# Windowed attention in a fused attention, MoE and FFT-FFN kernel: from two heads a product to rows of 128 queries of one head

## Chip, cores and metric

The kernel runs on one core of one Trainium2 chip. The metric is the device time of one execution in microseconds (us), the median of three runs.

## The reference

Three stages follow one another on inputs of 2 batches, 8 heads, 768 positions and head size 64. The change lies in the first:

```python
scores_l = scale * q @ k.T              # scale = 1/8; kept where |i-j| < 16, else -1e9
k_sum = k.reshape(B,H,24,32,D).max(3)   # one key for each block of 32
v_sum = v.reshape(B,H,24,32,D).mean(3)
scores_s = scale * (q . k_sum) + log(32)
a = softmax(concat([scores_l, scores_s], -1))   # sum + 1e-9 below the line
out = a @ concat([v, v_sum])
```

The second stage is a mixture of 8 experts (each token one expert, chosen by its logits or taken over from the token before it), the third a two-dimensional Fourier transform with a layer norm and a feed-forward network.

## The kernel before

**Attention** (`attention`, from L49). A unit u is a batch and four of its heads (hg); there are four units. A unit is cut into six steps c, a step into two blocks j of 64 queries, so that there are 24 steps t = 6u+c, each with 128 queries of four heads. A block of 64 queries needs 96 keys of its window and the 24 block keys, 120 in all. The loop at L208 runs over t and takes the phases of five steps at once, so that all engines have work:

- S1 (L123, TensorE) forms the scores of step t. Two heads share a product: their queries lie on the partitions 0 to 63 and 64 to 127 of a tile Q that is zero elsewhere, so one product has 128 rows of the contraction and 128 output rows (64 queries of the first head, 64 of the second) by 120 columns. There are four products a step; each shows as two weight loads and two matmuls in the trace.
- D1 (L130, VectorE) adds the mask and takes the negative maximum, four times a step on 128x120 (a custom instruction and one that reads its accumulator).
- A1 (L138, ScalarE) takes the exponential, four times.
- S3 (L144) transposes (four times), A3 (L149) copies the result to `att`.
- S4 (L151) multiplies by the values: four products of 128 columns of `att` by 130 columns (two heads, each with 64 values and a 1 that gives the sum). Only the half of each result that belongs to its own head is used.
- D4 (L159, VectorE) takes the reciprocals of the sums and scales: four reciprocals on 64x2 and four multiplications on 64x128.
- S5, A5, S6 (L178 to L190) transpose the finished rows and multiply them by the router's weights into the PSUM tile `big`.

At step t the TensorE does S1(t), S6(t-5), S3(t-2), S4(t-3) and S5(t-4), in this order; the VectorE does D1(t), then D4(t-3); the ScalarE A3(t-2), A5(t-4), A1(t). The queues run in program order. S1 has two PSUM buffers (`psc`), S4 three (`ppo`).

Around them lies the preparation of the next unit, set out by step in the tables PREP and LOADS (L203 to L205): `prep_q` copies the queries into Q (ScalarE, GpSimd), `prep_k` takes the block maxima (L98) and copies them behind each window (L99), both on the VectorE, `prep_v` adds up the values of a block (L109, GpSimd), and `prep_v2`, `prep_v3` bring them to their rows behind the values (L120). SyncE issues the loads of a unit one to five steps ahead. All of it needs the data of unit u+1 from DMA.

From step 13 on, pieces of the router's work (the generator `early`) are put between the VectorE's instructions by `ex.d()` and on the TensorE by `ex.p()`, up to eight and one a step. After step 28 the router's second part follows, in which the VectorE and TensorE answer each other, then the experts.

Of the kernel before, what the change touches and what calls it, by code (L numbers as in the profile page):

```python
# [15 lines left out]
def keep_warm(nc,I,ps,n):  # L16
    """matrix products without a use, that keep the tensor engine's clock up while it waits"""
    for _ in range(n): nc.tensor.matmul(ps,lhsT=I['busy'][:,0:128],rhs=I['busy'],start=True,stop=True)

def lay_attn(q,k,v,wg,wl):  # L20
    c=np.ascontiguousarray
    # b hg h2 d pair j q'
# [11 lines left out]
    band=(np.abs(qq+16-r)<16)  # L34
    m=np.full((3,128,120),np.log(32.0)*8,np.float32)
    for vi in range(3):
        bb=band.copy()
        if vi==1: bb&=(r>=16)
        if vi==2: bb&=(r<80)
        w=np.where(bb,0.0,-8e9)  # L40
        m[vi,:64,:96]=w; m[vi,64:,:96]=w
    mask=c(m.transpose(1,0,2))
# [6 lines left out]
def attention(tc,ctx,cp,I,ident,x_dram,plg,late,hook,ex):  # L49
    """plg psum [128,2hg,12,10]"""  # L50
    nc=tc.nc
    with tc.tile_pool(name="at2",bufs=2) as p2, tc.tile_pool(name="at1",bufs=1) as p1, \
         tc.tile_pool(name="at3",bufs=3) as p3, ExitStack() as pctx, \
         tc.tile_pool(name="pat",bufs=1,space=PSUM) as pat_, \
         tc.tile_pool(name="ppo",bufs=3,space=PSUM) as ppo_, tc.tile_pool(name="pxt",bufs=1,space=PSUM) as pxt_:
        px_=pctx.enter_context(tc.tile_pool(name="atx",bufs=1)); sctx=ExitStack(); psc_=sctx.enter_context(tc.tile_pool(name="psc",bufs=2,space=PSUM,side="right"))
        mask=p1.tile([128,3,120],F32,name="mask"); 
        wgl=p1.tile([128,4,10],F32,name="wgl"); 
        Q=[p1.tile([128,2,12,2,64],F32,name=f"Q{i}") for i in range(2)]
        nc.vector.memset(Q[0][0:64,:,:,1,:],0.0); nc.vector.memset(Q[0][64:128,:,:,0,:],0.0)  # L60
# [4 lines left out]
        kw={};vw={};vT={};qt={};KS={}  # L65
        kw[0]=p2.tile([128,2,12,120],F32,name="kw0",tag="kw",bufs=3)
        k0=p2.tile([128,2,12,120],F32,name="k0",tag="kw",bufs=3).rearrange("p a b c -> p (a b c)")[:,0:1664].rearrange("p (a b) -> p a b",a=2)
        def load(u,what):
# [18 lines left out]
        def prep_q(u,pr,h2,eng):  # L87
            s=slice(64*h2,64*h2+64); eng(Q[u%2][s,pr,:,h2,:],qt[u][s,pr])
        def prep_q0(js,k=0):
            for j in js:  # L90
                for h2 in range(2):
                    s=slice(64*h2,64*h2+64)
                    (nc.scalar.copy if (h2+k)%2==0 else nc.vector.tensor_copy)(Q[0][s,:,j,h2,:],qt[0][s,:,j])
        def prep_k(u,pr,half=None):
            o=slice(0,12) if half is None else slice(6*half,6*half+6)
            if half in (None,0): KS[u,pr]=p3.tile([128,24],F32,name=f"ks{u}_{pr}",tag="ks")
            ks=KS[u,pr]
            nc.vector.tensor_reduce(ks.rearrange("p (j t) -> p j t",j=12)[:,o],kw[u][:,pr,o,16:80].rearrange("p j (t r) -> p j t r",t=2),axis=AX.X,op=ALU.max)  # L98
# [12 lines left out]
        def prep_v2(u):
            pv=pxt_.tile([120,2,128],F32,name=f"pv{u}",tag="xt")
            for pr in range(2): nc.tensor.transpose(pv[:,pr,:],vs[u%3][:,pr,:],ident)
            vv=vss[u%2][96:120].rearrange("p (c e) -> p c e",e=65)[:,:,0:64]
            nc.scalar.mul(vv,pv[96:120].rearrange("p a (h d) -> p (a h) d",h=2),1.0/32)
            src=vss[u%2][96:121].unsqueeze(1)
            row=lambda j,k: vw[u][96:121,j:k].rearrange("p j c e -> p j (c e)")
            prep_v3(u,nc.scalar.copy,0,2)
        def prep_v3(u,eng,j,k):
            eng(vw[u][96:121,j:k].rearrange("p j c e -> p j (c e)"),vss[u%2][96:121].unsqueeze(1).to_broadcast([25,k-j,260]))  # L120
        xt={}; st={}
        NT=24
        def S1(t):  # L123
            u,c=divmod(t,6)
            sc=psc_.tile([128,512],F32,name=f"sc{t}",tag="sc")[:,0:480].rearrange('p (g k) -> p g k',g=4)
            for g in range(4):
                jj,pr=divmod(g,2); j=2*c+jj
                nc.tensor.matmul(sc[:,g,:],lhsT=Q[u%2][:,pr,j].rearrange('p a b -> p (a b)'),rhs=kw[u][:,pr,j,:],start=True,stop=True)
            st['s',t]=sc
        def D1(t):  # L130
            u,c=divmod(t,6); sc=st.pop(('s',t))
            e=p2.tile([128,4,120],F32,name=f"e{t}",tag="e"); nm=p3.tile([128,4],F32,name=f"nm{t}",tag="nm")
            for g in range(4):
                j=2*c+g//2; vi=1 if j==0 else 2 if j==11 else 0
                nc.vector.tensor_tensor_reduce(out=e[:,g,:],in0=sc[:,g,:],in1=mask[:,vi,:],scale=-0.125,scalar=1e30,op0=ALU.add,op1=ALU.min,accum_out=nm[:,g:g+1])
                if t>16: ex.d()
            st['e',t]=(e,nm)
        def A1(t):  # L138
            e,nm=st.pop(('e',t))
            a=p3.tile([128,4,120],F32,name=f"a{t}",tag="a")  # L140
            for g in range(4):
                nc.scalar.activation(a[:,g,:],e[:,g,:],AF.Exp,bias=nm[:,g:g+1],scale=-1.0)
            st['a',t]=a
        def S3(t):  # L144
            a=st.pop(('a',t))
            pa=pat_.tile([120,4,128],F32,name=f"pa{t}",tag="pa")
            for g in range(4): nc.tensor.transpose(pa[:,g,:],a[:,g,:],ident)
            st['pa',t]=pa
        def A3(t):  # L149
            nc.scalar.copy(att[t%2][0:120],st.pop(('pa',t)))  # L150
        def S4(t):  # L151
            u,c=divmod(t,6); b,hg=U[u]
            for jj in range(2):
                po=ppo_.tile([128,2,130],F32,name=f"po{t}_{jj}",tag="po")
                for pr in range(2):
                    j=2*c+jj
                    nc.tensor.matmul(po[:,pr,:],lhsT=att[t%2][0:121,2*jj+pr,:],rhs=vw[u][:,j,2*pr:2*pr+2,:].rearrange("p a b -> p (a b)"),start=True,stop=True)
                st['po',t,jj]=po
        def D4(t):  # L159
            u,c=divmod(t,6); b,hg=U[u]  # L160
            if hg==0: xt[(b,c)]=px_.tile([128,512],F32,name=f"xt{b}_{c}",tag=f"xt{c}")
            x=xt[(b,c)]
            xv=x.rearrange("p (g a h d) -> p g a h d",g=2,a=2,h=2)
            rs=p3.tile([128,2,2],F32,name=f"rs{t}",tag="rs")
            pos=[st.pop(('po',t,jj)) for jj in range(2)]
            for jj in range(2):
                for h2 in range(2):
                    s=slice(64*h2,64*h2+64)
                    nc.vector.reciprocal(rs[s,jj],pos[jj][s,:,65*h2+64])
            for jj in range(2):  # L170
                for h2 in range(2):
                    s=slice(64*h2,64*h2+64)
                    nc.vector.tensor_tensor(out=xv[64*jj:64*jj+64,hg,:,h2,:],in0=pos[jj][s,:,65*h2:65*h2+64],
                        in1=rs[s,jj].unsqueeze(2).to_broadcast([64,2,64]),op=ALU.mult)
                    if t>12: ex.d()
            if hg==1:
                nc.sync.dma_start(x_dram[b*896+c*128:b*896+c*128+128],x)
        def S5(t):  # L178
            u,c=divmod(t,6); b,hg=U[u]
            px=pxt_.tile([128,2,128],F32,name=f"px{t}",tag="xt")  # L180
            for i in range(2): nc.tensor.transpose(px[:,i,:],xt[(b,c)][:,hg*256+i*128:hg*256+i*128+128],ident)
            st['px',t]=px
        def A5(t):
            xT=p2.tile([128,2,128],F32,name=f"xT{t}",tag="xT")
            nc.scalar.copy(xT,st.pop(('px',t)))
            st['x',t]=xT
        def S6(t):
# [826 lines left out]
```

## Time and profile before

| | us |
|---|---|
| median of three runs | 624.75 |
| lowest, highest | 623.68, 631.16 |
| span of the profiled execution | 627.5 |

The profiled execution has no time of its own in the list; of the three runs only the one of 631.16 is as long as its span. The span runs from the first to the last instruction. The stages on it: attention up to 115 us, the router's second part to 148, experts to 283, transform to 346, feed-forward to the end. A duration in the trace is that of one instruction from its start to its end; matmuls overlap, so what one costs in a row is read from the distance of the starts.

### The profile page before, as it was taken

To read this page: it belongs to the slowest core of one execution; us is meant where nothing else is said; L and a number is where in the kernel's file an instruction comes from. 1 tells how busy PE (TensorE), PEld (TensorE's weight loads), DVE (VectorE), ACT (ScalarE), POOL (GpSimd) and SP (SyncE) were. 2 spreads that over 40 slices of the span, in tenths; PEclk is the share of its full clock that TensorE was granted. 3 is DMA by queue.
4 is the path that set the end of the run, shared out by engine and by line. 5 is a ranking of instruction groups with operands and counts; after the bars stand their busy time and mean duration, and the time that the engine had idled before them with its cause. 6 is when DMAs were issued, how large, how long until landed. Compare 5 with 4: busy or idle time off the path is not lost.

```text
span 627.5 us, 8719 instructions
## 1 busy us (share of the span) xinstructions
PE 574.5 (92%) x3154; PEld 487.1 (78%) x3154; DVE 388.8 (62%) x944; ACT 252.3 (40%) x472; POOL 159.1 (25%) x166
## 2 busy tenths in 40 slices
PE   7788788669999999996989999879999999999997
PEld 4688778658998899995858787657888888888885
DVE  5898988784989898882686999992311111311012
ACT  4675746424566767662425434444112111111000
POOL 5631225454044344331265323430000000000000
PEclk8897989889999999997978999998999999999999
DMA  8994305407898899923301434420100000100001
GB/s 253 335 324 168 111 6 217 184 21 281 304 341 271 332 361 309 311 110 103 135 0 33 153 117 134 145 91 1 67 1 1 0 2 0 68 0 1 0 1 67
DMA packets 21933, 84.05 MB, mean 134 GB/s; under 512 B 2782, under 2 KB 3294, under 8 KB 18304
## 3 DMA queue, kind: packets, MB, share of 16 engines
q1 hardware_dynamic: 18432, 72.62, 33.3%
q0 software_dynamic: 3456, 10.85, 4.9%
q8 instruction: 26, 0.43, 0.3%
q14 instruction: 19, 0.16, 0.1%
HBM read 73.23 MB, written 10.22 MB: 133 GB/s over the span
## 4 chain that ended last, share of the span: by engine, by line
PE 37%; DVE 15%; issue 1%; ACT 1%; SPq 0%; DMA 0%; DVEq 0%
PE fpy L923 16%; PE fph L912 15%; DVE ft L683 3%; DVE ft L684 2%; DVE ft L682 2%; PE s1q L800 1%; DVE fhl L915 1%; DVE st L727 1%; DVE ft L681 1%; PE lpt L756 1%; PE py L553 1%; PE ph L539 1%; PE s L800 1%; DVE cl L778 1%; PE pp L800 0%
## 5 line engine op out<-in xcount | busy, mean ns | idle before, releaser
L915 DVE SCALAR_TENSOR_TENSOR fhl<-fph,fhh 128x512 fp32r<-128x512 f32 x48 | 33.1, 689 | 143.7 <-ACT fhh L914 143.7
L914 ACT ACTIVATE fhh<-fph 128x512 fp32r<-128x512 f32 x48 | 28.6, 596 | 156.4 <-PE fph L912 156.4
L539 PE MATMUL ph<-xx,wh 128*128 128x256 f32 x448 | 84.4, 290 | 6.1 <-DMA dwr<-x_dram 6.1
L923 PE MATMUL fpy<-fwh,fhl 128*128 128x512 f32 x192 | 76.3, 397 | 6.2 <-DVE fhl L915 6.2
L539 PEld LDWEIGHTS ph<-xx,wh 128*128 128x128 f32 x448 | 72.3, 196 | 8.2 <-issue 6.5
L912 PE MATMUL fph<-unh,fwh 128*128 128x512 f32 x192 | 76.1, 396 | 0.0
L923 PE MATMUL fpy<-fwh,fhh 128*128 128x512 f32 x192 | 76.0, 396 | 0.0
L923 PE MATMUL fpy<-fwl,fhh 128*128 128x512 f32 x192 | 75.6, 394 | 0.0
L912 PE MATMUL fph<-unh,fwl 128*128 128x512 f32 x192 | 75.5, 393 | 0.0
L912 PE MATMUL fph<-unl,fwh 128*128 128x512 f32 x192 | 75.5, 393 | 0.0
L539 PE MATMUL ph<-xx,wl 128*128 128x256 f32 x224 | 64.5, 288 | 0.8 <-DVE wl L530 0.8
L530 DVE TENSOR_TENSOR wl<-wr,wh 128x1024 fp32r<-128x1024 f32 x47 | 55.4, 1220 | 12.5 <-ACT wh L529 12.5
L529 ACT CAST wh<-wr 128x1024 fp32r<-128x1024 f32 (+1 forms) x58 | 56.2, 1018 | 15.9 <-PE py L553 13.5
L689 POOL TENSOR_TENSOR fwl<-ft,fwh 128x512 fp32r<-128x512 f32 x32 | 43.2, 1351 | 75.1 <-ACT fwh L688 75.0
L923 PEld LDWEIGHTS fpy<-fwh,fhl 128*128 128x128 f32 x192 | 36.3, 189 | 16.6 <-DVE fhl L915 8.8
L553 PE MATMUL py<-wh,hl 128*128 128x512 f32 x112 | 44.6, 398 | 4.8 <-DVE hl L544 4.8
L539 PEld LDWEIGHTS ph<-xx,wl 128*128 128x128 f32 x224 | 44.3, 198 | 1.2 <-DVE wl L530 1.2
L553 PE MATMUL py<-wh,hh 128*128 128x512 f32 x112 | 45.2, 404 | 0.0
L553 PE MATMUL py<-wl,hh 128*128 128x512 f32 x112 | 44.2, 394 | 0.0
L923 PEld LDWEIGHTS fpy<-fwl,fhh 128*128 128x128 f32 x192 | 36.5, 190 | 8.1
L912 PEld LDWEIGHTS fph<-unh,fwl 128*128 128x128 f32 x192 | 36.0, 188 | 8.5
L923 PEld LDWEIGHTS fpy<-fwh,fhh 128*128 128x128 f32 x192 | 36.5, 190 | 7.8
(293 smaller groups left out, 1067.8 us busy)
## 6 DMA issues: line engine op xcount, KB each, us to landing
wr<-in_wm SPq DMA_DIRECT2D x28, 1024.0 KB, 6.2
fr<-in_wc SPq DMA_DIRECT2D x32, 512.0 KB, 3.6
vw<-in_vw SPq DMA_DIRECT2D x8, 585.0 KB, 9.3
kw<-in_kw SPq DMA_DIRECT2D x6, 720.0 KB, 9.7
vT<-in_vT SPq DMA_DIRECT2D x4, 768.0 KB, 8.3
x_dram<-xt SPq DMA_DIRECT2D x12, 256.0 KB, 2.1
dwr<-x_dram SPq DMA_DIRECT2D x12, 256.0 KB, 4.6
out<-dwr SPq DMA_DIRECT2D x12, 256.0 KB, 2.1
```

The lines of the kernel that those rows point to most:

```text
L529: S.copy(wh[:,o],raw[:,o])
L530: eng[i%2].tensor_tensor(out=wl[:,o],in0=raw[:,o],in1=wh[:,o].bitcast(F32),op=ALU.subtract)
L539: T.matmul(H[s,c][:,fb],lhsT=a[:,o],rhs=b[:,kd],start=n==0,stop=n==11); n+=1
L553: T.matmul(PY[s][tt],lhsT=a[:,fb,q],rhs=b[:,o],start=(c==0 and fb==0 and i==0),stop=(c==3 and fb==1 and i==2))
L682: V.tensor_scalar(out=ti,in0=ti,scalar1=4,scalar2=1,op0=ALU.logical_shift_left,op1=ALU.logical_shift_right)
L683: V.scalar_tensor_tensor(out=ti,in0=raw[:,:,0],scalar=29,in1=ti,op0=ALU.logical_shift_right,op1=ALU.bitwise_or)
L684: V.scalar_tensor_tensor(out=ti,in0=raw[:,:,1],scalar=-2147483648,in1=ti,op0=ALU.bitwise_and,op1=ALU.bitwise_or)
L689: nc.gpsimd.tensor_tensor(out=l[:,k],in0=t,in1=h[:,k].bitcast(F32),op=ALU.subtract)
L912: T.matmul(ph,lhsT=a[:,kd,o],rhs=x[:,kd],start=n==0,stop=n==11); n+=1
L914: S.activation(hh,ph,AF.Relu)
L915: V.scalar_tensor_tensor(out=hl,in0=ph,scalar=0.0,in1=hh.bitcast(F32),op0=ALU.max,op1=ALU.subtract)
L923: T.matmul(PY[c][t],lhsT=a[:,q],rhs=b[:,k],start=f==0 and i==0,stop=f==15 and i==2)
```

## The change

Rows are now 128 queries of one head, from two blocks: a result tile has the first block's 64 queries on the partitions 0 to 63 and the second's on 64 to 127.

- S1: Q and its zeros are gone, the queries are used as loaded. Two bf16 products (69 rows by 240 columns) write the mask and the log(32) of the block keys into the scores' PSUM tile, one for each h2 and bank; then eight products of 64 contraction rows, 64 output rows and 120 columns, each in one quarter of the array, are added.
- D1: one maximum over 128x480 and one multiplication by -1/8 on 128x4. A1 reads the scores from PSUM.
- S4: eight products of 64 columns of `att` by 65 columns, into one PSUM tile. D4: one reciprocal on 128x4, one multiplication on 128x256.
- PSUM: the scores take two banks a buffer (four in all), S4's result one buffer in place of three.
- `prep_q` and its copies are gone, and so are the memsets of Q. The queries have two buffers in place of one. `prep_k` is one maximum a pair (steps 2 and 3 of a unit), its copy `prep_k2` goes to GpSimd (steps 3 and 4, the second behind `prep_v`). `prep_v3` goes to GpSimd but for one piece at step 2. The mask's load stands second in the queue, its cast to bf16 is a new VectorE instruction at the start.

```diff
+        def prep_k(u,pr):
+            ks=KS[u,pr]=p3.tile([128,24],F32,name=f"ks{u}_{pr}",tag="ks")
+            V.tensor_reduce(ks.rearrange("p (j t) -> p j t",j=12),kw[u][:,pr,:,16:80].rearrange("p j (t r) -> p j t r",t=2),axis=AX.X,op=ALU.max)
+        def prep_k2(u,pr): G.tensor_copy(kw[u][:,pr,:,96:120],KS[u,pr].unsqueeze(1).to_broadcast([128,12,24]))
...
         def S1(t):
-            for g in range(4):
-                jj,pr=divmod(g,2); j=2*c+jj
-                nc.tensor.matmul(sc[:,g,:],lhsT=Q[u%2][:,pr,j].rearrange('p a b -> p (a b)'),rhs=kw[u][:,pr,j,:],start=True,stop=True)
+            sc=psc_.tile([128,2,512],F32,name=f"sc{t}",tag="sc")[:,:,0:240].rearrange('p h (g k) -> p h g k',g=2)
+            for h2 in range(2):
+                T.matmul(sc[:,h2],lhsT=maskb[:,128*var:128*var+128],rhs=maskb[:,384:504].unsqueeze(1).to_broadcast([69,2,120]),start=True,stop=False)
+            for pr in range(2):
+                for h2 in range(2):
+                    s=slice(64*h2,64*h2+64)
+                    for jj in range(2):
+                        T.matmul(sc[64*jj:64*jj+64,h2,pr],lhsT=qt[u][s,pr,2*c+jj],rhs=kw[u][s,pr,2*c+jj],start=False,stop=pr==1)
...
         def D1(t):
-                nc.vector.tensor_tensor_reduce(out=e[:,g,:],in0=sc[:,g,:],in1=mask[:,vi,:],scale=-0.125,scalar=1e30,op0=ALU.add,op1=ALU.min,accum_out=nm[:,g:g+1])
+            V.tensor_reduce(mx,sc,axis=AX.X,op=ALU.max)
+            if t>16: ex.d(); ex.d()
+            V.tensor_scalar(out=nm,in0=mx,scalar1=-0.125,scalar2=None,op0=ALU.mult)
...
         def S4(t):
+            po=ppo_.tile([128,4,65],F32,name=f"po{t}",tag="po")
+            for g in range(4):
+                for jj in range(2):
+                    T.matmul(po[64*jj:64*jj+64,g],lhsT=att[t%2][0:121,g,64*jj:64*jj+64],rhs=vw[u][:,2*c+jj,g],start=True,stop=True)
...
         def D4(t):
+            V.reciprocal(rs,po[:,:,64])
+            V.tensor_tensor(out=x.rearrange("p (g e d) -> p g e d",g=2,e=4)[:,hg],in0=po[:,:,0:64],in1=rs.unsqueeze(2).to_broadcast([128,4,64]),op=ALU.mult)
...
+        PREP={2:(('k',0),),3:(('k',1),('k2',0)),4:('v',('k2',1))}
+        LOADS={2:((1,'v'),(1,'w'),(2,'k')),5:((2,'q'),(2,'v')),8:((2,'w'),(3,'k')),11:((3,'q'),(3,'v')),14:((3,'w'),)}
```

How this moves the queues, first the TensorE at step 5 (sc is S1's result, big S6's, pa S3's, po S4's, px S5's), before:

```order
L128 MATMUL sc_400<-kw_152,Q_141 128x120 x4
L190 MATMUL big<-wgl,xT_384 128x10 x2
L147 MATMUL pa_407<-ident,a_336 120x128 x4
L157 MATMUL po_0_412<-vw_174,att_145 128x130 x2
L157 MATMUL po_1_415<-vw_174,att_145 128x130 x2
L181 MATMUL px_426<-ident,xt_1_373 128x128 x2
```

and now:

```order
L116 LDWEIGHTS maskb
L116 MATMUL sc_402<-maskb 128x240
L116 LDWEIGHTS maskb
L116 MATMUL sc_402<-maskb 128x240
L121 MATMUL sc_402<-kw_150,qt_163 64x120 x8
L174 MATMUL big<-wgl,xT_384 128x10 x2
L140 MATMUL pa_415<-ident,a_341 120x128 x4
L149 MATMUL po_420<-vw_171,att_142 64x65 x8
L165 MATMUL px_433<-ident,xt_1_379 128x128 x2
```

The order of the phases stays; 16 products become 26, eight of them in quarters and eight in halves of the array, with full-array products between the two kinds.

The VectorE from the end of D1(5) over D4(2) into D1(6) (e, nm from D1, rs and xt from D4), before:

```order
L135 ISA e_420,nm_421<-sc_400,mask 128x120
L135 ISA nm_421 128x1
L169 RECIPROCAL rs_430<-po_0_412 64x2 x2
L169 RECIPROCAL rs_430<-po_1_415 64x2 x2
L173 TENSOR_TENSOR xt_2_429<-po_0_412,rs_430 64x2x64 x2
L173 TENSOR_TENSOR xt_2_429<-po_1_415,rs_430 64x2x64 x2
L135 ISA e_467,nm_468<-sc_449,mask 128x120
```

and now D1(4), D4(1), D1(5), D4(2):

```order
L126 TENSOR_REDUCE mx_372<-sc_347 128x4
L128 TENSOR_SCALAR nm_373<-mx_372 128x4
L156 RECIPROCAL rs_380<-po_363 128x4
L158 TENSOR_TENSOR xt_1_379<-po_363,rs_380 128x256
L126 TENSOR_REDUCE mx_429<-sc_402 128x4
L128 TENSOR_SCALAR nm_430<-mx_429 128x4
L156 RECIPROCAL rs_437<-po_420 128x4
L158 TENSOR_TENSOR xt_2_436<-po_420,rs_437 128x256
```

Sixteen VectorE instructions a step have become four.

GpSimd between the block sums of units 0 and 1 (vs is the end of prep_v, kw the windows of unit 1), before:

```order
L110 TENSOR_TENSOR vs_147<-vT_172 128x2x24
L241 MEMSET Q_142 64x24x64 x2
L88 COPY Q_142<-qt_221 64x12x64
L109 TENSOR_TENSOR vT_264<-vT_264 128x768
```

and now:

```order
L101 TENSOR_TENSOR vs_144<-vT_169 128x2x24
L109 COPY vw_171<-vss_147 25x1560
L90 COPY kw_220<-ks_0_290 128x12x24
L100 TENSOR_TENSOR vT_262<-vT_262 128x768
L100 TENSOR_TENSOR vT_262<-vT_262 128x384
L100 TENSOR_TENSOR vT_262<-vT_262 128x192
L100 TENSOR_TENSOR vT_262<-vT_262 128x96
L101 TENSOR_TENSOR vs_145<-vT_262 128x2x24
L90 COPY kw_220<-ks_1_338 128x12x24
```

The block keys of unit 1's second pair (the last row) now stand behind the sums over that unit's values.

## Rows read from the trace of the kernel before

**Rows 1.** Busy time by stage: the first steps, then steps 6 to 23.
```profile
core 0: us, PE busy (x) PEld busy (x) DVE busy (x) ACT busy (x) POOL busy (x), PEclk, DMA share, GB/s
0.00:33.00 33.00, 24.93 (x145) 19.11 (x145) 23.44 (x90) 18.95 (x43) 18.25 (x36) 0.90 0.95 300
33.00:104.00 71.00, 58.69 (x454) 55.63 (x453) 62.97 (x330) 43.95 (x118) 19.29 (x26) 0.90 0.46 158
```
**Rows 2.** Timeline at D1(6), D1(23) and the router's first instruction after the attention.
```profile
33.02 0.28 DVE L135 CUSTOM_DVE_ANT_0 e<-sc,mask 128x120 f32<-128x120 f32 x1
...
103.65 0.28 DVE L135 CUSTOM_DVE_ANT_0 e<-sc,mask 128x120 f32<-128x120 f32 x1
...
114.76 0.22 DVE L321 TENSOR_TENSOR rlg<-rlg,big 128x60 f32<-128x60 f32 x1 [0.41 <-PE big L190]
```
**Rows 3.** Timeline of the VectorE, one step (start, us, then as above).
```profile
26.05 0.28 DVE L135 CUSTOM_DVE_ANT_0 e<-sc,mask 128x120 f32<-128x120 f32 x1
...
26.86 0.76 DVE L169 RECIPROCAL rs<-po 64x2 f32<-64x2 f32 x4
27.66 1.25 DVE L173 TENSOR_TENSOR xt<-po,rs 64x128 f32<-64x128 f32 x4
```
**Rows 4.** Timeline of the TensorE, one step at full clock.
```profile
65.30 0.38 PE L181 MATMUL px<-ident,xt 128*128 128x128 f32 x2
65.52 1.05 PE L128 MATMUL sc<-kw,Q 128*128 128x120 f32 x8
66.41 0.52 PE L190 MATMUL big<-wgl,xT 128*128 128x10 f32 x4
66.78 0.63 PE L147 MATMUL pa<-ident,a 128*120 128x128 f32 x4
67.25 1.06 PE L157 MATMUL po<-vw,att 121*128 121x130 f32 x8
68.14 0.38 PE L181 MATMUL px<-ident,xt 128*128 128x128 f32 x2
```
**Rows 5.** Groups by shape, 0 to 210 us: busy us, mean ns.
```profile
L98 DVE TENSOR_REDUCE ks<-kw 128x12 f32<-128x384 f32 x12 | 6.6, 552 | 0.3
L102 DVE TENSOR_REDUCE ks<-k 128x24 f32<-128x768 f32 x2 | 1.9, 953 | 1.0 <-DMA k<-in_k 0.9
L513 DVE TENSOR_TENSOR xx<-pt,xx 128x512 fp32r<-128x512 f32 x8 | 5.4, 686 | 2.4 <-ACT xx L512 2.4
L104 POOL COPY kw<-k 128x384 f32<-128x384 f32 x2 | 1.0, 502 | 4.1 <-DMA k<-in_k 4.1
```
**Rows 6.** Timeline of the TensorE in the transform: products over 128 and over 33 rows.
```profile
302.08 1.22 PE L800 MATMUL s<-ft,Pd 128*128 128x386 f32 x6
303.14 0.52 PE L814 MATMUL s<-ft,Pd 128*2 128x386 f32 x2
303.50 0.69 PE L800 MATMUL s<-ft,Pd 128*128 128x386 f32 x3
304.12 0.44 PE L815 MATMUL s<-fr,rP 33*128 33x386 f32 x1
304.49 0.79 PE L800 MATMUL s<-ft,Pd 128*128 128x386 f32 x3
```
**Rows 7.** Timeline of GpSimd: block sums of unit 1.
```profile
27.04 4.03 POOL L109 TENSOR_TENSOR vT<-vT 128x768 f32<-128x768 f32 x4 [5.08 <-DMA vT<-in_vT]
31.15 0.29 POOL L110 TENSOR_TENSOR vs<-vT 128x48 f32<-128x48 f32 x1
```
**Rows 8.** Timeline, VectorE beside GpSimd, and the same line later.
```profile
78.44 2.35 POOL L120 COPY vw<-vss 25x2600 f32<-25x2600 f32 x1 [12.17 <-ACT vss L115]
78.50 2.31 DVE L328 TENSOR_TENSOR val<-cf,r 128x6 bf16<-128x6 f32 x1
...
120.12 0.17 DVE L328 TENSOR_TENSOR val<-cf,r 128x6 bf16<-128x6 f32 x1
```
**Rows 9.** Timeline of the TensorE, S1 at a lower clock.
```profile
53.52 1.90 PE L128 MATMUL sc<-kw,Q 128*128 128x120 f32 x8
```

More of the change, by code (lines that the diff above doesn't have):

```diff
@@ L33, in lay_attn @@
     qq=np.arange(64)[:,None]; r=np.arange(96)[None]
[L34 to L42, printed above, removed]
+    mm=np.zeros((69,120),np.float32); mm[:64,:96]=np.where(np.abs(qq+16-r)<16,0.0,-8e9)
+    part=np.float32(np.log(32.0)*8)
+    for i in range(3):
+        hi=(np.float32(part).view(np.uint32)&np.uint32(0xFFFF0000)).view(np.float32); mm[64+i,96:]=hi; part=np.float32(part-hi)
+    mm[67,:16]=-8e9; mm[68,80:96]=-8e9
+    ml=np.zeros((69,3,128),np.float32); ml[:64]=np.concatenate([np.eye(64)]*2,1)[:,None]; ml[64:67]=1.0
+    ml[67,0,:64]=1.0; ml[68,2,64:]=1.0
+    mask=c(np.concatenate([ml.reshape(69,384),mm],1))
     wgl=np.zeros((512,10),np.float32); wgl[:,:8]=wg; wgl[:,8:9]=wl
@@ L74, in load @@
             if 'q' in what:
-                qt[u]=p2.tile([128,2,12,64],F32,name=f"qt{u}",tag="qt",bufs=1)
+                qt[u]=p2.tile([128,2,12,64],F32,name=f"qt{u}",tag="qt",bufs=2)
                 if u:
@@ L114, in prep_v2 @@
             vv=vss[u%2][96:120].rearrange("p (c e) -> p c e",e=65)[:,:,0:64]
[L115 to L118, printed above, removed]
+            S.mul(vv,pv[96:120].rearrange("p a (h d) -> p (a h) d",h=2),1.0/32)
+            prep_v3(u,S.copy,0,2)
         def prep_v3(u,eng,j,k):
@@ L146, in S3 @@
             pa=pat_.tile([120,4,128],F32,name=f"pa{t}",tag="pa")
-            for g in range(4): nc.tensor.transpose(pa[:,g,:],a[:,g,:],ident)
+            for g in range(4): T.transpose(pa[:,g,:],a[:,g,:],ident)
             st['pa',t]=pa
         def A3(t):
-            nc.scalar.copy(att[t%2][0:120],st.pop(('pa',t)))
+            S.copy(att[t%2][0:120],st.pop(('pa',t)))
         def S4(t):
[L152 to L158, printed above, removed]
+            u,c=divmod(t,6)
+            po=ppo_.tile([128,4,65],F32,name=f"po{t}",tag="po")
+            for g in range(4):
+                for jj in range(2):
+                    T.matmul(po[64*jj:64*jj+64,g],lhsT=att[t%2][0:121,g,64*jj:64*jj+64],rhs=vw[u][:,2*c+jj,g],start=True,stop=True)
+            st['po',t]=po
         def D4(t):
@@ L161, in D4 @@
             if hg==0: xt[(b,c)]=px_.tile([128,512],F32,name=f"xt{b}_{c}",tag=f"xt{c}")
[L162 to L175, printed above, removed]
+            x=xt[(b,c)]; po=st.pop(('po',t))
+            rs=p3.tile([128,4],F32,name=f"rs{t}",tag="rs")
+            V.reciprocal(rs,po[:,:,64])
+            if t>12: ex.d(); ex.d()
+            V.tensor_tensor(out=x.rearrange("p (g e d) -> p g e d",g=2,e=4)[:,hg],in0=po[:,:,0:64],in1=rs.unsqueeze(2).to_broadcast([128,4,64]),op=ALU.mult)
+            if t>12: ex.d(); ex.d()
             if hg==1:
@@ L217, in attention @@
             else: at_(S3,t-2); at_(S4,t-3); at_(S5,t-4); at_(S6,t-5)
-            todo=PREP.get((min(u,1),c),()) if t<NT and u<3 else ()
-            for w in todo:
-                if w[0]=='k': prep_k(u+1,*w[1:])
+            todo=PREP.get(c,()) if t<NT and u<3 else ()
             at_(D1,t)
@@ L226, in attention @@
             at_(D4,t-3)
+            for w in todo:
+                if w[0]=='k': prep_k(u+1,*w[1:])
             at_(A3,t-2)
```

100 lines of the change are left out of this document (34 added, 66 removed).

## The prediction

> **What bounds the kernel now.** Start with the busy time by stage. In steps 6 to 23 of the attention the VectorE is busy for 62.97 of 71 us and the TensorE for 58.69, at a mean granted clock of 0.90 [rows 1]. Then look for the place where the steps are paced: D1(6) starts at 33.02 and D1(23) at 103.65, so 17 steps take 70.63 us, 4.155 each [rows 2]. Of a step the VectorE needs at least 2.89: from the first instruction of D1 (26.05) to its reciprocals (26.86) it is 0.81, the four reciprocals take 0.80 to the next start, the four multiplications 1.25, and 0.03 follow [rows 3]. The rest up to 4.155 is the preparation of the next unit, the router's pieces, and waits between the two engines. The TensorE's own work is shorter: with the clock full and no wait one step goes from 65.30 to 68.14, 2.84 us, cut by the starts into S5 0.22, S1 0.89, S6 0.37, S3 0.47, S4 0.89 [rows 4]. So before the change the VectorE paces these steps, and the TensorE has 1.3 us a step to spare.
>
> What comes after the attention hangs on its end: the router's second part starts at 114.76 with the last S6 [rows 2], and the experts after it. A microsecond won or lost in the attention is one of the whole. A result that differs by less than 2%, 12.5 us, can hardly be told from no change.
>
> **The change, part by part.**
>
> *VectorE.* D1 becomes one maximum over 480 columns. The same operation took 552 ns on 384 and 953 on 768 [rows 5], which makes 0.65 here. Scaling 128x4 and the reciprocal are small operations, about 0.17 each as the 0.17 of L328 [rows 8]. The multiplication on 256 columns lies between the 0.31 of one of four on 128 [rows 3] and 686 ns on 512 [rows 5]: 0.42. Sum 1.41 in place of 2.89. The copies of `prep_k` and most of `prep_v3` leave this engine too. Saved: about 1.5 us in each of 24 steps, 36 us of busy time. That is not 36 us of the result, since the TensorE is late next, and it gets more to do.
>
> *TensorE.* S5, S6 and S3 stay: 0.22 + 0.37 + 0.47 = 1.06. Four things are new.
>
> The mask: two products of 240 columns. Six of 386 columns follow each other within 1.06, 0.177 each [rows 6]; by columns 0.11 each, 0.22 for both.
>
> S1: eight products, which will show as 16 records as four showed as 8. A record of S6 has 10 moving columns and still costs 0.37/4 = 0.09, one of S1 with 120 costs 0.11, one of S4 with 130 also 0.11 [rows 4]. So what is streamed hardly matters, and the 128 columns of weights do. Now each record loads 64 columns. If the load halves, 16 records cost 0.89; if a record keeps its 0.11, 1.78; if besides quarters of the array work beside each other, 0.45. The trace of before has no product in such quarters. I take 1.0, near the row of S1 with half the load, a little more because 120 columns still have to be streamed.
>
> S4: also 16 records, 64 columns of weights and 65 moving columns; the bounds are the same, 0.45 to 1.78. I take 0.89.
>
> Changes of shape: in the transform a product over 33 rows stands between products over 128. From 303.50 to 304.49 there are four records, 0.99, where 0.177 each would make 0.71: 0.28 for going there and back [rows 6]. A step now goes there and back twice (mask to quarters to S6; S3 to halves to S5). Between 0 and 0.9; I take 0.6.
>
> Here the Trainium skill speaks against the change: "TensorEngine Tiling (Array Packing)", Key Properties, says that a change of the tiling mode, not of the tile alone, drains the engine. The trace agrees, with the 0.28 above. The same page's Theoretical Speedup holds out up to two times for each dimension of at most 64; no run here shows that yet, and it is the first rival below.
>
> Sum of a step: 1.06 + 0.22 + 1.0 + 0.89 + 0.6 = 3.77 us. The VectorE (1.41 and at most eight router pieces of 0.17 to 0.3) and the ScalarE (43.95 us over these steps, 2.6 each with the queries' copies that now go [rows 1]) stay below it. So the steps turn from VectorE-paced to TensorE-paced, and 17 of them take 64.1 in place of 70.63: 6.5 won. By the bounds the TensorE's step is 2.2 to 5.7; below about 2.6 the ScalarE paces, so 2.6 to 5.7.
>
> *The first steps.* The copies of the queries and the memsets go, but D1(6) can't move by much. DMA is busy for 0.95 of the first 33 us [rows 1], so an earlier issue of the queries (two buffers) brings nothing to land earlier, and nearly as many bytes come first. The maxima for unit 1 now stand on the VectorE at step 2, before D1(3), and wait there for that unit's keys. And S1(6) now waits for `prep_k2(1,1)`, which on GpSimd is queued behind the block sums: these waited for their data until 27.04 and ended at 31.15 + 0.29 = 31.44 [rows 7]. A copy on GpSimd took 0.5 for 384 columns [rows 5], so the second half of S1(6) starts at about 31.9 and D1(6) at 32.6: 0.4 won, whatever the steps before it do. The cost is bounded by 0 and 1. In the later units the data lie ready steps ahead.
>
> *The last steps* (103.65 to 114.76 [rows 2]). Before, D4 at 2.1 us a step paces them. Now D4 is 0.6, but S3, S4, S5, S6 with one change there and back take 2.25 on the TensorE, so only the chain behind the last step gets shorter: D4 by 1.45, D1 by nothing worth naming. I take 2.0, bounds 0 and 3.
>
> *Work on GpSimd.* A small VectorE instruction (L328, 0.17 later) lasted 2.31 while GpSimd copied 25x2600, ending with it [rows 8]. The new scaling of 128x4 could be held in the same way by three such copies and by parts of the sums, at most 2.3 each time. The TensorE is two buffers ahead, so most of it is hidden behind S1 of the next step; cost 0, at most 5, and I keep that for the range.
>
> Sum: 6.5 + 0.4 + 2.0 = 8.9 us. The profiled execution's span is 627.5, 2.75 above the median of 624.75; the difference carries over, so 624.75 - 8.9 = 615.9 us. Between the bounds: at 2.6 a step 26.4 + 0.4 + 3 = 30 won (595); at 5.7 it is 26.3 lost, less 0.4 (651).
>
> **Rivals.**
>
> *Quarters and halves side by side.* S1 0.45, S4 0.45, changes 0.3: the TensorE would need 1.06 + 0.22 + 1.2 = 2.5, and the ScalarE's 2.6 with some waits makes about 2.9. Won: 17 x 1.25 + 0.4 + 2.5 = 24, 601 us. For it: consecutive products name other quarters, and nothing in the program orders them. Against: each record loads weights first, and the 0.11 of a record looks like a load [rows 4].
>
> *The records keep their price* (this one ends on the other side). A product over a quarter costs what one over the whole array does, 0.11 a record, and each change its 0.28 in a pair or more. The step is then 1.06 + 0.22 + 1.78 + 1.78 + 0.6 = 5.4, which loses 17 x 1.28 = 22 and wins back 0.4; the last steps win nothing: 646 us. From 4.3 us a step on the change is a loss (4.155 and the 2.4 won elsewhere over 17), from 5.0 a loss over 2%. For it: twice as many instructions, and short products don't get cheaper with fewer moving columns, as S6 shows.
>
> *The clock stays low.* At the lower granted level S1 took 1.90 in place of 1.05 [rows 4, 9]. Before, that cost little since the VectorE paced; now it would cost at once. If the drains and the small products bring a quarter of the 17 steps to 1.2 GHz, that is 17 x 3.77 / 4 = 16 lost, and with the 8.9 won 632 us. Against it: the TensorE will have fewer waits than now, where the mean was 0.90.
>
> *The relief isn't there.* If other waits, not the VectorE's work, make up the 4.155, the steps stay at it and only 2.4 are won: 622 us.
>
> **Chances.** The forecast (3.4 to 4.4 a step) 0.40, side by side 0.32, kept price 0.14, clock 0.07, no relief 0.07. Faster by over 2% (below 612.3) takes all of the second and a little of the first: 0.35. Slower by over 2% (above 637.2) takes the kept price and a part of the clock: 0.17. Within: 0.48. The likeliest case alone spans 605 to 628. The range that should hold 8 in 10 is 599 to 639.
>
> **What would show it.** D1(6) near 32.6 and D1(23) near 97. A step of the TensorE without waits at 3.8, with S1 from its first mask product to S6 at 1.5 and S4 at 1.2, changes included. Idle time of the VectorE before D1 ended by TensorE in nearly every step, where before it waited three or four times in all. S1(6)'s second half released by GpSimd. If a record of S1 follows the last one within 0.03, the first rival is right; if at 0.11, the second. If the clock falls below 0.8 in stretches where the TensorE doesn't wait, the third. The forecast is wrong if the steps stay paced by the VectorE, or if the gain comes from the first or last steps.

## The result and the profile after

The changed kernel took 609.76 us in the median of four executions (604.23 to 615.4), the kernel before 625.05 in four (623.68 to 631.16) beside it. The ratio is 0.971, 95% interval 0.965 to 0.977: faster by 2.9%. The ratios here and below leave out executions that took over 1.5% longer than the fastest of their kernel. The prediction was 615.9 us, no difference that can be told (0.48), with 0.35 for faster. The time lies in its range, but what was called likelier than faster did not come.

The profiled execution took 606.48 us, span 604.7. First the busy time by stage (columns: length, busy time of PE, PEld, DVE, ACT and POOL, TensorE's granted clock, share of the DMA, GB/s):

```profile
0.00:33.00 33.00, 22.30 (x218) 12.53 (x223) 13.08 (x27) 13.60 (x36) 16.40 (x36) 0.85 0.95 292
33.00:45.00 12.00, 12.00 (x114) 9.26 (x116) 3.70 (x10) 5.11 (x15) 2.35 (x1) 0.56 0.41 163
45.00:87.40 42.40, 41.83 (x668) 32.58 (x664) 31.33 (x102) 31.90 (x96) 19.31 (x27) 1.00 0.67 220
```

Against [rows 1] the bound has changed sides. From 45 us on the TensorE is busy for 41.83 of 42.40 us and the VectorE for 31.33. The middle row is one that nobody planned for: 12 us in which the TensorE is busy throughout, at little more than half the clock.

One step of the TensorE at full clock, the row that answers to [rows 4]:

```profile
50.96 0.44 PE L165 MATMUL px<-ident,xt 128*128 128x128 f32 x2
51.23 0.37 PE L116 MATMUL sc<-maskb 69*128 69x240 bf16 x2
51.53 0.64 PE L121 MATMUL sc<-kw,qt 64*64 64x120 f32 x16
52.10 0.61 PE L174 MATMUL big<-wgl,xT 128*128 128x10 f32 x4
52.57 0.63 PE L140 MATMUL pa<-ident,a 128*120 128x128 f32 x4
53.13 0.69 PE L149 MATMUL po<-vw,att 121*64 121x65 f32 x16
53.75 0.44 PE L165 MATMUL px<-ident,xt 128*128 128x128 f32 x2
```

From start to start: S5 0.27, mask 0.30, the quarters of S1 0.57, S6 0.47, S3 0.56, S4 0.62, in all 2.79 us where 3.77 was predicted. The changes of shape are inside these figures. They show where the weight loads stand idle with nothing to wait for that the profile shows ("issue"): before the quarters, before S6 and before the halves of S4:

```profile
51.53 0.41 PEld L121 LDWEIGHTS sc<-kw,qt 64*64 64x64 f32 x16 [0.20 <-issue]
52.10 0.52 PEld L174 LDWEIGHTS big<-wgl,xT 128*128 128x128 f32 x4 [0.16 <-issue]
53.13 0.55 PEld L149 LDWEIGHTS po<-vw,att 121*64 121x64 f32 x16 [0.17 <-issue]
```

On the VectorE, groups of the stretch from 45 to 87 us and the waits from 45 to 87.4 (in total, times, longest):

```profile
L126 DVE TENSOR_REDUCE mx<-sc 128x4 f32<-128x480 f32 x14 | 9.2, 654 | 2.8 <-PE sc L121 2.5
L158 DVE TENSOR_TENSOR xt<-po,rs 128x256 f32<-128x256 f32 x15 | 6.3, 417 | 0.3
L128 DVE TENSOR_SCALAR nm<-mx 128x4 f32<-128x4 f32 x14 | 5.6, 398 | 1.0
L156 DVE RECIPROCAL rs<-po 128x4 f32<-128x4 f32 x15 | 2.7, 180 | 6.2 <-PE po L149 6.2
...
DVE rs L156 <- PE po L149: 6.2, 11, 0.9
DVE mx L126 <- PE sc L121: 2.8, 8, 0.5
```

The maximum (0.65), the multiplication (0.42) and the reciprocal (0.18) have the predicted price. The VectorE now waits for the TensorE 19 times, in 11 of the 15 steps from D1(9) to D1(23). Only the scaling (0.17 when alone) is dearer in the mean: at 47.66 it lasted 1.68 us, while GpSimd added from 47.50 to 49.31, and at 64.99 once more 1.68.

The first steps, from the timeline of several engines:

```profile
21.32 0.95 DVE L89 TENSOR_REDUCE ks<-kw 128x24 f32<-128x768 f32 x1 [4.38 <-DMA kw<-in_kw]
24.59 0.69 PE L149 MATMUL po<-vw,att 121*64 121x65 f32 x16 [2.98 <-DVE xt L158]
28.12 4.00 POOL L100 TENSOR_TENSOR vT<-vT 128x768 f32<-128x768 f32 x4 [4.84 <-DMA vT<-in_vT]
32.91 0.68 PE L121 MATMUL sc<-kw,qt 64*64 64x120 f32 x8 [1.94 <-POOL kw L90]
33.66 0.66 DVE L126 TENSOR_REDUCE mx<-sc 128x4 f32<-128x480 f32 x1 [3.62 <-PE sc L121]
```

The chain is the one predicted for S1(6): data, block sums, copy, quarters. But it came a microsecond later (D1(6) at 33.66, not 32.6), and the maxima that the change moved up (L89) waited 4.38 us for their keys. D1(3) and D4(0) stand behind them, and S4(1) needs the one buffer that D4(0) reads, so that it waited 2.98. Behind that wait the clock fell (TensorE by windows: busy, clock, DMA share, GB/s):

```profile
24.00:26.00 2.00, 1.41 (x28) 1.00 1.07 243
26.00:28.00 2.00, 2.00 (x24) 0.60 0.97 206
...
42.00:44.00 2.00, 2.00 (x23) 0.63 0.02 4
44.00:46.00 2.00, 2.00 (x32) 1.00 0.03 8
```

The end of the attention, which answers to [rows 2]:

```profile
87.33 0.66 DVE L126 TENSOR_REDUCE mx<-sc 128x4 f32<-128x480 f32 x1 [0.34 <-PE sc L121]
...
98.16 0.22 DVE L292 TENSOR_TENSOR rlg<-rlg,big 128x60 f32<-128x60 f32 x1
```

The books, before less after: D1(6) 33.02 - 33.66 = 0.64 lost; 17 steps 70.63 - (87.33 - 33.66) = 17.0 won; the last steps 11.11 - 10.83 = 0.3 won. That is 16.6 us at L292. From there to the end of the span the profiled execution of before took 512.7 us, that of after 506.5. The kernel wasn't changed there. The same stretch took 507 to 517 us in the profiled executions of the runs below that compute the same results, so I count these 6 us as the two profiled executions' own and not as the change's. The medians differ by 15.3 us and the ratio makes 18; the 16.6 lie between.

### The profile page after: what moved, and what is told of

It reads as the page before. It is cut to its first block, busy times and chain, and to the rows that moved or that the text cites. A ratio compares the mean times of both kernels' runs of the same rounds, so it can differ in the third digit from the quotient of the medians.

```text
span 604.7 us, 9247 instructions
## 1 busy us (share of the span) xinstructions
PE 563.1 (93%) x3585; PEld 462.9 (77%) x3586; DVE 345.4 (57%) x635; ACT 240.9 (40%) x460; POOL 160.8 (27%) x170
## 4 chain that ended last, share of the span: by engine, by line
PE 37%; DVE 16%; ACT 1%; issue 1%; DMA 1%; SPq 0%; DVEq 0%
PE fpy L894 16%; PE fph L883 16%; DVE ft L654 4%; DVE ft L655 2%; DVE ft L653 2%; PE s1q L771 1%; DVE fhl L886 1%; DVE st L698 1%; DVE ft L652 1%; PE lpt L727 1%; PE s L771 1%; PE py L524 1%; DMA dwr<-x_dram 1%; DVE cl L749 1%; PE pp L771 1%
## 5 line engine op out<-in xcount | busy, mean ns | idle before, releaser
L510 PE MATMUL ph<-xx,wh 128*128 128x256 f32 x448 | 82.3, 285 | 2.1 <-DVE eps L737 2.1
L510 PEld LDWEIGHTS ph<-xx,wh 128*128 128x128 f32 x448 | 70.7, 191 | 4.3 <-issue 2.5
L894 PEld LDWEIGHTS fpy<-fwh,fhl 128*128 128x128 f32 x192 | 36.3, 189 | 16.6 <-DVE fhl L886 8.8
```

The lines of the kernel that those rows point to most:

```text
L510: T.matmul(H[s,c][:,fb],lhsT=a[:,o],rhs=b[:,kd],start=n==0,stop=n==11); n+=1
L894: T.matmul(PY[c][t],lhsT=a[:,q],rhs=b[:,k],start=f==0 and i==0,stop=f==15 and i==2)
```

## The experiments

A product in fp32 shows as two matmul records in the trace. Theory A says that the parts of the array work beside each other, that the TensorE's step of 2.79 paces, and that the VectorE's relief lets this show. Theory B says that the records got cheap because their loads and streams are half as long. A second question is what the start costs. Times are medians, and ratios are against the kernel before, timed beside each run (the changed kernel: 0.971, 0.965 to 0.977).

**1. The same part in a row.** S1's loops become `h2, jj, pr`, S4's `jj, g`.

> The same products as in the changed kernel with the same results, in another order: the two products of a quarter follow each other in S1, and all four of a half in S4, where in the changed kernel the next product always names another part. Theory A (the parts work beside each other, so that the next product starts before the last one ends): the quarters of S1 go from 0.57 us to 0.8 to 1.0, S4 from 0.62 to 0.9 to 1.1, the step from 2.79 to 3.2 to 3.5, the whole 8 to 16 us longer than the changed kernel. Theory B (a record is cheap only because its load and its stream are half as long; the order plays no part): both stay within 0.05, the whole within 2 us of the changed kernel.

```profile
51.90 0.97 PE L149 MATMUL po<-vw,att 121*64 121x65 f32 x16
52.80 0.44 PE L165 MATMUL px<-ident,xt 128*128 128x128 f32 x2
...
53.38 0.66 PE L121 MATMUL sc<-kw,qt 64*64 64x120 f32 x16
53.97 0.61 PE L174 MATMUL big<-wgl,xT 128*128 128x10 f32 x4
```

S4 went from 0.62 to 0.90, as A said; the quarters stayed at 0.59, as B said. The whole took 613.28 us, ratio 0.978 (0.971 to 0.986). The step of 3.10 and the 3.5 us more in the whole lie below what A expected. So the order matters for eight records in a row on a half and not for four in a row on a quarter; why not for the quarters, this run doesn't show, and it doesn't decide between A and B for them.

**2. One quarter.**

```
-T.matmul(sc[64*jj:64*jj+64,h2,pr],lhsT=qt[u][s,pr,2*c+jj],rhs=kw[u][s,pr,2*c+jj],start=False,stop=pr==1)
+T.matmul(sc[0:64,h2,pr],lhsT=qt[u][0:64,pr,2*c+jj],rhs=kw[u][0:64,pr,2*c+jj],start=True,stop=True)
```

The masks' products end their sums with `stop=True`, so the quarters overwrite the mask.

> All eight products of S1 name the same quarter of the array (rows 0 to 63, columns 0 to 63); this leaves out the scores of the second head of each pair and those of the second window. Everything else stays, the number of records too. Theory A (side by side): S1's quarters go from 0.57 us to 1.0 to 1.8, the step to 3.2 to 4.0, the whole 10 to 28 us longer than the changed kernel. Theory B (half the load): 0.57 stays within 0.1, the whole within 3 us.

```profile
51.63 1.85 PE L121 MATMUL sc<-kw,qt 64*64 64x120 f32 x16
53.41 0.61 PE L174 MATMUL big<-wgl,xT 128*128 128x10 f32 x4
```

The same 16 records took 1.78 us, 0.111 each, in place of 0.57, and the step 4.00. Shape, count and columns are the same, so B can't explain the 0.57, and A can. It is also the prediction's upper bound to the digit: on its own quarter a record costs what a record of the whole array did. In the changed kernel a quarter gets four of the 16 records, 4 x 0.111 = 0.44, and I take the remaining 0.13 for the change of shape. D1(23) came at 102.54, which is nearly the 103.65 of the kernel before. The whole, 781.88, can't be compared, because wrong scores go into the router: from its first instruction to the end the profile has 663.6 us in place of 506.5.

**3. The VectorE's part undone**: four maxima, four reciprocals and four multiplications on 64 partitions.

> The VectorE's part of the change is undone alone: four maxima over 120 columns, four reciprocals and four multiplications on 64 partitions a step; the TensorE's part stays. Theory A (the TensorE's cheap parts are worth something only because the VectorE was relieved): VectorE 1.0 + 0.17 + 0.8 + 1.25 = 3.2 us a step, which paces; with the maxima of the next unit and the router's pieces 3.4 to 3.8, the whole 10 to 18 us longer than the changed kernel. Rival (the gain is the TensorE's alone): within 3 us of the changed kernel.

```profile
51.84 0.69 PE L149 MATMUL po<-vw,att 121*64 121x65 f32 x16 [1.57 <-DVE xt L161]
...
70.00:80.00 10.00, 7.50 (x97) 6.17 (x98) 9.41 (x37) 5.11 (x18) 4.84 (x7) 0.85 0.46 145
80.00:110.00 30.00, 29.96 (x275) 22.51 (x274) 21.11 (x115) 13.98 (x40) 9.98 (x15) 0.50 0.22 82
```

The whole took 637.57 us, ratio 1.022 (1.016 to 1.028): slower than before the change, and more than A expected. In the first window the VectorE paces (9.41 of 10). Then the clock is at half for 30 us and the TensorE paces with the same products. So the new products without the relief are a loss here; how much of it is the VectorE's and how much the clock's, the run doesn't separate. That the relief pays only while the products are short is seen in run 2: there the VectorE was relieved, the quarters of S1 took 1.78, and of the gain 1.1 us were left at D1(23).

**4. S4 twice** (`for g in (0,1,2,3,0,1,2,3)`).

> S4 is computed twice over, with the same result: 16 records more a step, 0.55 to 0.62 us. Theory A (the TensorE paces the steps): the step goes from 2.79 to 3.35 to 3.45, the whole 12 to 15 us longer than the changed kernel. Rival (the ScalarE, the VectorE or waits pace them): under 5 us.

```profile
52.52 1.15 PE L149 MATMUL po<-vw,att 121*64 121x65 f32 x32
53.61 0.44 PE L165 MATMUL px<-ident,xt 128*128 128x128 f32 x2
```

S4 is 1.09 in place of 0.62: 16 more records cost 0.47, eight to each half, 0.058 each. The step is 3.26, so the TensorE paces. Yet the whole was 613.51 us, ratio 0.982 (0.976 to 0.988), some 4 us longer and not the 11 that 24 x 0.47 makes. From D1(9) to D1(23), at full clock in both, the 14 steps took 46.38 us in place of 40.42, which is 0.43 more each, as it should be. But D1(6) to D1(9) took 10.23 in place of 13.25: there the clock was 0.76 between 30 and 40 us and 1.00 after, in the changed kernel 0.50 and 0.83.

**5. Two changes of shape more** (one mask, its four quarters, the other mask, its four).

> The products of S1 in another order with the same result: mask of one head, its four quarters, mask of the other head, its four quarters. That is one more change there and back a step, and quarters of only one row half in a row. Theory A (each change of shape costs what stands as idle time before the loads of the quarters, 0.16 to 0.20 us): step 2.79 to 3.1 to 3.2, the whole 4 to 9 us longer than the changed kernel. Theory B (a change costs nothing, the 0.2 is the latency of the masks' last columns): step within 0.08, the whole within 2 us.

```profile
89.66 0.27 PE L116 MATMUL sc<-maskb 69*128 69x240 bf16 x1
89.86 0.63 PE L120 MATMUL sc<-kw,qt 64*64 64x120 f32 x8
90.42 0.28 PE L116 MATMUL sc<-maskb 69*128 69x240 bf16 x1
90.62 0.63 PE L120 MATMUL sc<-kw,qt 64*64 64x120 f32 x8
```

S1 with its masks, to S6 at 91.18, is 1.52 in place of 0.87, the step 3.44 at full clock; twice what was expected. Most of it isn't the change: each group of eight records has only two quarters, four records for each, and takes 0.56, as long as 16 records with four for each of four quarters (0.57). So it is the busiest quarter that counts. Here no two products write the same place, as they do in run 2, so that alone doesn't make its records dear. Of the 0.65 more, the second group's records are 0.44, and 0.21 are left for the two changes, some 0.1 each. The times went from 616.53 to 672.0 (median 635.24, no ratio): in the profile the clock was at half from 32 to 82 us, 6.08 a step.

**6. and 7. The start.** In 6 `4:('v',('k2',1))` becomes `4:(('k2',1),'v')`. In 7 also the first unit gets `{3:(('k',0),),4:(('k',1),('k2',0),('k2',1),'v')}`.

> On GpSimd the copy of the second half of the next unit's maxima (prep_k2(u,1)) goes ahead of the block sums (prep_v), not behind them. Theory (S1(6) waits 1.94 us for that copy, which is queued behind sums that wait for their own data): D1(6) at 31.0 to 32.0 in place of 33.66, and the whole 1.5 to 4 us shorter, more where the clock then recovers earlier. Rival (what is won there is lost again at the next wait for data): D1(12) within 0.5 us of the changed kernel's 55.0 and the whole within 1 us.

> As the last one, and in the first unit the two maxima over the next unit's keys stand a step later each (steps 3 and 4 in place of 2 and 3), so that D1(3) isn't queued behind one that waits for its keys (4.38 us on the VectorE). Theory: D1(3) at 20.5 to 21.8 in place of 23.04, the TensorE's wait of 2.98 us before S4(1) gone, D1(6) at 29.5 to 31.5, steps 6 to 9 at 2.8 to 3.3 us each since the clock doesn't fall; the whole 4 to 9 us shorter. Rival (data bound these steps whatever the order): D1(6) after 32.5, the whole within 1.5 us of the last one.

6: The wait before S1(6) is gone. D1(6) came at 32.37, a little later than expected; the clock stood at half from 19 to 31 us here, behind a wait of 2.55 us that ended at 17.37. D1(23) came at 83.71 in place of 87.33, and the whole took 610.37 us, ratio 0.964 (0.957 to 0.972), which can't be told from the changed kernel. 7: D1(3) came at 19.49 and D1(6) at 26.21, 7.4 us earlier, better than expected. Then a wait stood where the theory had none, `prep_v2` at step 7, behind the same sums:

```profile
32.16 0.68 PE L104 MATMUL pv<-ident,vs 128*120 128x128 f32 x2 [2.20 <-POOL vs L101]
...
34.00:64.00 30.00, 30.00 (x266) 22.88 (x266) 11.09 (x26) 12.58 (x39) 6.89 (x9) 0.50 0.65 230
```

The TensorE was busy for all of these 30 us at half clock, 4.99 a step. The whole took 613.44 us (600.16 to 621.24): nothing won in the median, though the shortest is 4 us below the changed kernel's shortest.

**8. Products without a use in the waits** (20 before S4(1), 12 before S1(6)).

> Products without a use fill two waits of the TensorE at the start: 20 of 256 columns before S4(1), where it waited 2.98 us, and 12 before S1(6), where it waited 1.94; nothing else is changed. Theory (steps 5 to 9 are long because the clock fell behind those waits): D1(6) stays within 1 us of 33.66, the granted clock between 30 and 45 us is over 0.9 in place of 0.50 to 0.83, D1(9) at 42 to 43.5 in place of 46.9, the whole 3 to 6 us shorter. Rival (those steps wait for data at either clock): D1(9) within 1 us, the whole within 1.5 us.

The forecast failed. The clock stayed at 1.00 until 32 us, but GpSimd's sums began at 29.17 in place of 28.12, with their data, S1(6) waited the longer (D1(6) at 34.70), and the clock fell there:

```profile
33.96 0.68 PE L124 MATMUL sc<-kw,qt 64*64 64x120 f32 x8 [3.55 <-POOL kw L90]
```

D1(9) came at 47.62, the whole took 612.35 us, ratio 0.974 (0.967 to 0.981): no gain. As the clock wasn't held, the run doesn't tell whether it makes steps 5 to 9 long; run 9 does.

**9. to 12. Without the wait.** Run 9 is run 7 with `prep_v2` and `prep_v3` of the second unit at step 8, not 7. Run 10 is run 9 with `late()`, the transfers of zeros and constants, at step 3 in place of 1. Run 11 is run 9 with S6, S3, S1, S4 in this order from step 4 on, and `prep_v2` behind S4. Run 12 is the changed kernel again.

> As the kernel with the maxima moved and the copy first, and prep_v2 of the second unit a step later (step 8 in place of 7), so that the TensorE isn't queued behind the block sums (2.20 us at 29.96, after which the clock stood at 0.50 until 64). Theory (the low clock comes behind the waits for the second unit's data, and is the larger part of the price of the start): no wait of the TensorE over 1 us between 20 and 45 us, the granted clock 1.00 there, D1(9) at 34 to 36, D1(23) at 74 to 78 in place of 87.3, the whole 8 to 14 us shorter than the changed kernel. Rival (the next wait for data takes its place): D1(23) after 82, the whole within 4 us of the changed kernel.

> As the last one, and the loads of late() (the zeros of one block of x and the constants, 0.46 MB) are issued at step 3 in place of 1, behind those of the second unit's values. Theory (the sums wait for bytes that stand ahead in the queues: 0.46 MB of the 300 GB/s are 1.5 us): GpSimd's L100 at 26.5 in place of 27.7 to 28.1, D1(23) up to 1 us earlier than in the last one. Rival: no difference, since by then nothing waits for those sums.

> As the first of this call, and the TensorE's step in the order S6, S3, mask, quarters, halves, S5 from step 4 on, so that S4 follows S1 directly: three changes of shape a step in place of four, the same products. Theory (a change costs the 0.16 to 0.2 us that stand before the loads): step 2.79 to 2.6, the whole 2 to 4 us shorter than the first of this call. Rival (going from quarters to halves costs two changes, or S3 now waits for the ScalarE): step not under 2.75, the whole within 1.5 us or longer.

> The changed kernel once more, nothing edited, on the same chip as the three others. Both theories: 604 to 616 us. If the spread of its times comes from how long the clock stays low after the first waits, its profile shows either a low stretch between 25 and 45 us like the first one or a longer one with a longer time; if it comes from elsewhere, the step times up to D1(23) agree within 1 us with the first profile whatever the time.

9, by windows:

```profile
20.00:30.00 10.00, 9.47 (x163) 7.22 (x163) 9.16 (x18) 7.12 (x21) 4.62 (x5) 1.00 1.03 299
30.00:40.00 10.00, 9.35 (x144) 7.46 (x141) 6.86 (x17) 7.98 (x24) 5.18 (x7) 1.00 1.02 338
40.00:79.00 39.00, 37.15 (x586) 28.72 (x584) 26.75 (x94) 28.55 (x86) 19.43 (x27) 1.00 0.70 233
```

The clock is full from 20 to 79 us, and no wait of the TensorE between 20 and 45 us is over 1.3. D1(6) to D1(9) took 8.84 us in place of 13.25. D1(9) came at 36.17 and D1(23) at 78.99, both a little later than expected, the second 8.3 us earlier than in the changed kernel. The whole took 601.63 us, ratio 0.956 (0.948 to 0.964). It is the best of the kernels; its interval ends where that of the changed kernel begins.

10: the sums began at 26.88, near what was expected, and D1(9) came 1.2 us earlier. But all of it stands at D1(2) already (15.94 against 17.16), and two profiles of the changed kernel, both with `late()` at step 1, differ there by as much (16.09, and 17.34 in run 12), so it can't be laid to the loads. Then the clock dropped to 0.66 between 60 and 70 us, behind a wait of 1.20 us for the last unit's sums, where 9 had the same wait (1.19) and kept its clock (the line of 10, then that of 9):

```profile
60.78 0.43 PE L104 MATMUL pv<-ident,vs 128*120 128x128 f32 x2 [1.20 <-POOL vs L101]
...
61.96 0.43 PE L104 MATMUL pv<-ident,vs 128*120 128x128 f32 x2 [1.19 <-POOL vs L101]
```

D1(23) came at 80.45, the whole took 609.54 us, ratio 0.969 (0.961 to 0.977). Nothing won.

11: a miss. One change of shape fewer is worth 0.09 (S3 takes 0.47 in place of 0.56), and the step became 3.38, because S6 now stands right behind S5 and waits for the ScalarE's copy between them. 628.04 us, ratio 0.996 (0.990 to 1.001), is more than this step makes: from 40 to 50 us the clock was 0.53 and from 60 to 100 between 0.64 and 0.68, so that the 17 steps took 78.48 us, 4.62 each.

```profile
52.70 0.44 PE L165 MATMUL px<-ident,xt 128*128 128x128 f32 x2
53.65 0.61 PE L174 MATMUL big<-wgl,xT 128*128 128x10 f32 x4 [0.52 <-ACT xT L169]
```

12: 611.27 us in the median of eight, 604.28 to 643.24, ratio 0.970 (0.963 to 0.977) without the three longest. Its profiled execution took 642.6, and the windows show why (below them the wait of S1(6)):

```profile
30.00:35.00 5.00, 2.69 (x26) 0.78 0.99 359
35.00:45.00 10.00, 10.00 (x88) 0.50 0.23 92
45.00:110.00 65.00, 65.00 (x578) 0.50 0.41 132
...
32.31 0.43 PE L121 MATMUL sc<-kw,qt 64*64 64x120 f32 x8 [3.76 <-POOL kw L90]
```

The waits stand at the same places as in the first profile with other lengths, 1.28 ahead of S4(1) and 3.76 ahead of S1(6). Behind the second the clock fell, and here it stayed at half to D1(23) at 119.46 us, 32.1 later than in the first profile, with a TensorE that was busy throughout.

## Why the prediction was right or wrong

*What bounds the kernel before, and the turn to the TensorE:* right. The VectorE's prices were right to 0.02 us but for the held scaling, the step is paced by the TensorE (run 4), and the VectorE waits for it in 11 of 15 steps. Run 3 rules out the rival "the relief isn't there".

*The TensorE's step:* here it failed. The step that failed is the pair of terms "S1: I take 1.0" and "S4: I take 0.89", with 0.6 for changes of shape on top. S1 and S4 measured 0.57 and 0.62, and this with the changes before them included, so the step is 2.79 and not 3.77. I had read "0.11 a record" off [rows 4] as a load that half the columns would halve, and put the overlap of quarters only in the bounds. The reading was wrong twice: a record on a quarter keeps its 0.111 though it loads 64 columns in place of 128 (run 2), and S1's whole gain comes from four quarters at once. A record of S4, also with 64 columns of weights, does cost less, 0.058 (run 4): the price seems to go with the columns streamed, 120 and 65, rather than with the weights, though no run changed one alone. So 0.89 was about right for S4's records in a row (0.90 in run 1), and the two halves at once make the rest. The sum that fits is the records of the busiest part, 4 x 0.111 for S1 and 8 x 0.058 for S4, and a remainder of 0.13 and 0.16, which I take for the change. Against [rows 4] with 0.89 each, S1 and S4 together win 0.6, nearly all of which (0.54) the mask (0.30) and the dearer neighbours take back: S5, S6 and S3 measured 1.30, not 1.06. So the step stays near its 2.84, and the gain in the steps is that the VectorE no longer holds them at 4.155.

*Changes of shape:* the "0.6" stood on top. Three places of 0.16 to 0.20 show before the loads, so the sum is about right, but removing one (run 11) gave 0.09 and adding two (run 5) 0.21. Their price by themselves stays open between 0.1 and 0.2 each.

*The first rival, side by side,* had the mechanism and the step (2.9, measured 2.79), and 601 us, 24 won. At L292 16.6 are won: of what is missing 4.3 lie in the 17 steps, 2.2 behind them and 1.0 before them. In the steps the third rival, "the clock stays low", came true from 5 to 8: D1(6) to D1(9) took 46.91 - 33.66 = 13.25 us for three steps, at 2.79 they would be 8.4. Not all of these 4.9 us come back where the clock holds: in run 9 the 17 steps took 51.66 us, 2.0 less than here, since D1(9) to D1(23) took 42.82 in place of 40.42. I had argued against this rival that the TensorE would have fewer waits. It has fewer later. At the start it has more: where the kernel before waited 2.18 us ahead of S4(1) and 0.50 ahead of S1(6), the changed one waited 2.98 and 1.94 (run 12: 1.28 and 3.76).

*That the time lies in the range is in part luck.* The forecast step was 0.98 too long, 16.7 us over 17 steps. At 2.79 they would have won 23.2, and 17.0 came; the first and the last steps brought 1.0 and 1.7 less than forecast. So errors of 9.0 us the other way hide over half of the first. The span of the likeliest case, 605 to 628, is also not what 3.4 to 4.4 a step make: with the bounds for the first and last steps it is 608 to 629.

*The first steps:* the chain through `prep_k2` was right, its size a microsecond off, and the sign too (0.4 won; 0.64 lost; in run 12 D1(6) stood at 32.81, 0.2 won). The wait of the maxima before D1(3) I named and gave no price; it was 4.38 on the VectorE and 2.98 on the TensorE. Runs 7 and 9 show what it was worth together with the wait of S1(6): in run 9 D1(23) is 8.3 us earlier. That D1(6) can't move by much, since the DMA is busy, was wrong: in run 7 it came 7.4 us earlier with the same loads in the same order, so the order of the engines' queues held it.

*The last steps:* 2.0 forecast, 0.3 measured. D4 did shorten the VectorE's chain, from D1(23) to the end of the last D4 8.21 us in place of 9.38, but 2.62 follow up to L292 in place of 1.73. I take the one buffer for S4's result (S4 waited 0.50 for D4 at 92.67) and the ScalarE's copies for the reason why no more is won; I made no run on this, and it stays open.

*GpSimd's hold on the scaling* (0, at most 5): seen, 0.40 in the mean against 0.17 alone, and hidden as argued: from 45 to 87.4 us the TensorE's waits add up to 0.3. It was not tried by itself.

## What to carry to other kernels

For products on parts of the array, count the records of the busiest part and multiply by what one costs in a row on it (here 0.111 us with 120 columns streamed, 0.058 with 65), then add the change of shape; alternate the parts. Before an engine is made the bound, look for the waits at its front that cost nothing until then, for now they can cost their own length and a low clock behind them. When one wait goes, the next wait for the same data takes its place (runs 7 and 9), so follow the data to the last instruction that needs it.

## What was not expected of the hardware

The clock. In both profiles of the changed kernel and in those of runs 1 and 3 to 8 it fell in or shortly behind a wait of the TensorE of 2 to 4 us in the first 36 us. Runs 2, 9 and 10, where no wait from 20 to 45 us was over 1.3, kept it full there. Later it fell in runs 3, 10 and 11 behind waits of 0.9 to 1.6 us. The clock then stayed at half for 17 us in the first profile (26 to 43, with the wait of 1.94 us inside), for 34 in run 7 and for 92 in run 12 (33 to 125), which is the same program as the first, and from the end of its wait on the TensorE of runs 7 and 12 was busy throughout. What ends such a stretch these runs don't show, nor whether a wait brings one: behind one of 1.2 us the clock fell in run 10 and held in run 9. At half clock the step is 4.99 in place of 2.79, and this is most of the spread from 604 to 643 us: of the 36.1 us between the two profiled executions of the changed kernel 32.1 stand at D1(23).

Small products were a surprise too: 16 records of fp32 in 0.57 us over four quarters and 1.78 on one, with 16 loads of weights in 0.41 us among them.
